# Attention kernel with a static instruction order: charging TensorE's tiling switches in the order's model, fillers in the tiling of their neighbours, projections through one bank, and the last unit by Ln and Exp

## The chip, the cores and the metric

The kernel runs on one core of one Trainium2 chip. The metric is the device time of one execution in microseconds (us). Every ratio compares runs of both kernels on the same chip in alternating rounds.

An execution is marked slow when it is over 1.5% above the fastest of the same kernel. With one core, that is the only sign of it. The granted TensorE clock in these traces is either 1.0 or 0.5 of full speed. I therefore use a second measure throughout, the **half-clock time** of an execution: twice (1 − mean granted clock) times the span. It says for how many microseconds TensorE ran at half speed.

Engines: TensorE (PE: matmuls; PEld: its weight loads), VectorE (DVE), ScalarE (ACT), GpSimd (POOL), SyncE (SP, issues the DMAs).

## The reference

Two attention layers on 2048 rows of width 512 with 32 heads of 16, outputs side by side. A is softmax attention and nearly all of the work. B is linear attention with softmax feature maps.

```python
def _A_ref(x, wqkv, wo):                      # x [1,2048,512] bf16
    qkv = (x @ wqkv).reshape(B, S, 3, H, Dh).transpose(2, 0, 3, 1, 4)
    q, k, v = qkv[0], qkv[1], qkv[2]
    p = softmax(einsum("bhqd,bhkd->bhqk", q, k) * Dh ** -0.5)
    o = einsum("bhqk,bhkd->bhqd", p, v)
    return o.transpose(0, 2, 1, 3).reshape(B, S, D) @ wo
# _B_ref (cut): phi = [softmax(x w_phi), softmax(-x w_phi)] for q and k;
#               o = phi_q (phi_k^T v) / (phi_q sum(phi_k) + 1e-6); o @ wo
return concatenate([a, b], axis=-1)
```

## The kernel before

Python decides the order of all instructions of every engine in advance. Each piece of work is a task with a modelled duration. A list scheduler takes the task that can start first and appends its instructions to its engine's list. Semaphores make the result correct whatever the true durations are, but the order is frozen: where the model is wrong, engines wait.

```python
    # in the scheduler: placing a task
        if self.filler is not None and t.eng == "pe":
            self.filler(self.free["pe"], start)      # zeros to keep TensorE busy
        t.end = start + t.dur + t.lat
        self.free[t.eng] = start + t.dur
```

A *unit* is 4 heads times 512 queries, and there are 32 units. Each unit has 16 key blocks. QK uses row tiling (4 row groups of 32), PV column tiling (4 groups of 32 columns), everything else the full array:

```python
    # QK: two row groups, one matmul each (a half-block of 1024 scores a partition)
    e.matmul(PS[:, b, :], KT[32*r:32*r+32, g, ...], QT[32*r:32*r+32, c, ...], start=True, stop=True,
             tile_position=(32 * r, 0))
    return _Task("pe", 0.3, pe_group(2, mm), ...)
    # PV: four column groups into bank 6; row 16 of each group becomes the softmax sum
    e.matmul(PS[32*r:32*r+32, 6, :], lhs(...), rhs(r), ..., tile_position=(0, 32 * r))
    t = _Task("pe", 0.25, emit, deps + ([xev[u - 1]] if u else []), ...)
```

The exponential of a half-block is made on one of two engines. On ScalarE it is one Exp into one of 7 score tiles `pT` (banks 0 to 3). On VectorE it is one conversion `rg<-PS` and then passes `rg<-rg` (the D banks, 4 and 5). The PV of a unit cannot start before the previous unit's bank 6 has been copied to X.

A filler puts zero matmuls, always on the full array, into the gaps that the model foresees on TensorE:

```python
    def fill(f, start):
        gap = start - f - 0.1
        ... # bank 6 while a PV group is open, else bank 7 if free
        while gap > 0.08:
            n = min(512, int((gap - 0.03) / 0.0004167) // 128 * 128)
            ... e.matmul(PS[:, bank, 0:n], zmv[:], rhs, ...)
            gap -= n * 0.0004167 + 0.03
```

The later K and Q projections run in pairs through both D banks, paced from 40 us on, one each 9 us. A unit ends with the division by its sums. The sums go out to DRAM, come back in another layout, a reciprocal is taken, it goes out and comes back broadcast, and GpSimd multiplies. Four output blocks follow, each through one bank, and then a check that all sums were in range, which writes a flag. The end of the program reads the flag and branches over a general version.

```python
            p1 = ... d_sum[u] <- X[16:128:32]        # 4 DMAs and a reciprocal
            p2 = ... Cs <- d_sum[u];   rc = reciprocal
            p3 = ... d_rec <- Cs;      p4 = ... Yd <- d_rec, broadcast
            mul[u] = ... pool: OT[:, g, :] = X * Yd
            if g == NG - 1: out_proj(c)              # 4 x (8 matmuls, copy, DMA), one bank
    ... # after the schedule: load all sums, three counts, flag
```

## Time and profile before

951.53 us, the median of 3 runs (951.09 to 953.96).

| stretch | length | what bounds it |
|---|---|---|
| body: start to the end of the last softmax Exp | 903.8 us | TensorE and ScalarE together to 700 us, then ScalarE |
| tail: from there to the end | 49.0 us | one serial chain |

First the busy times of the kernel before by stretch. The columns are the stretch, its length, busy time and (count) of PE, PEld, DVE, ACT and POOL, then the granted clock, the DMA share and GB/s.

```profile
core 0: us, PE busy (x) PEld busy (x) DVE busy (x) ACT busy (x) POOL busy (x), PEclk, DMA share, GB/s
40.00:100.00 60.00, 58.56 (x375) 15.93 (x378) 31.18 (x35) 49.61 (x55) 6.10 (x4) 1.00 0.02 6
...
300.00:400.00 100.00, 95.65 (x895) 27.84 (x900) 78.61 (x101) 83.61 (x98) 16.02 (x10) 0.95 0.05 14
...
700.00:800.00 100.00, 98.98 (x859) 27.25 (x859) 83.64 (x103) 97.85 (x107) 5.38 (x4) 1.00 0.06 18
```

TensorE looks full everywhere, but its fillers count as busy. ScalarE, whose work has no filler, is at 83% to 90% in the middle and 98% or more from 700 us on. VectorE is at 52% between 40 and 100 us.

The costliest groups of the kernel before (line, engine, operation, tiles, shapes, count; then busy us and mean ns of one; then idle time of the engine before them and what ended it):

```profile
L697 ACT ACTIVATE pT<-PS 128x1024 bf16<-128x1024 f32 x792 | 746.2, 1063 | 67.7 <-PE PS L595 47.4
...
L718 DVE TENSOR_SCALAR rg<-PS 128x1024 uint16<-128x1024 f32 x232 | 281.6, 1214 | 68.1 <-PE PS L587 67.2
...
L628 PE MATMUL PS<-zmv 128*128 128x512 bf16 (+3 forms) x498 | 145.9, 353 | 1.1 <-DVE zb L847 0.6
```

Of the 1024 half-blocks, 792 go to ScalarE and 232 to VectorE. From the waits list of ScalarE (total us, times, longest):

```profile
ACT pT L697 <- PE PS L595: 47.4, 18, 9.9
ACT pT L697 <- PE PS L587: 15.4, 38, 1.1
```

The 18 waits on PV (L595) are stalls with all seven score tiles full.

What a switch of tiling costs can be read off the timeline of the kernel before (start, duration shown, engine, line). The shown durations of matmuls overlap (0.40 us is shown where the next one starts after 0.32), so the starts are what to read:

```profile
501.44 0.40 PE L587 MATMUL PS<-QT,KT 32*128 32x512 bf16 x4
501.77 0.28 PE L628 MATMUL PS<-zmv 128*128 128x256 bf16 x1
501.98 0.39 PE L587 MATMUL PS<-QT,KT 32*128 32x512 bf16 x2
502.30 0.40 PE L595 MATMUL PS<-pT,VP 128*32 128x512 bf16 x4
```

From QK to PV is 0.32 us, where full-array fillers of 512 columns that follow each other start 0.215 us apart: about 0.1 us went into the change. The four QK matmuls on four row groups ran at once: the next matmul started 0.33 us after them, not four times 0.215. The 256-column filler took 0.21 us for about 0.107 us of streaming, half of the 0.215.

Last, the tail of the kernel before, from the timeline:

```profile
904.73 0.69 DVE L648 COPY X<-PS 128x512 f32<-128x512 f32 x1 [8.26 <-PE PS L595]
905.45 0.50 SPq L656 DMA_DIRECT2D d_sum<-X  x1
...
911.27 0.55 SPq L669 DMA_DIRECT2D Yd<-d_rec  x1
916.40 1.26 POOL L675 TENSOR_TENSOR OT<-X,Yd 128x512 bf16<-128x512 f32 x1 [18.80 <-DMA Yd<-d_rec]
...
918.12 3.91 PE L771 MATMUL PS<-WOp,OT 128*128 128x512 bf16 x7 [13.44 <-POOL OT L675]
...
922.07 0.69 DVE L775 CAST OA<-PS 128x512 bf16<-128x512 f32 x1 [13.08 <-PE PS L771]
...
933.85 0.69 DVE L775 CAST OA<-PS 128x512 bf16<-128x512 f32 x1 [2.70 <-PE PS L771]
...
935.33 0.39 SPq L1065 DMA_DIRECT2D sums<-d_sum  x1
...
941.81 2.29 DVE L1071 TENSOR_SCALAR_CACHE_REDUCE zb<-statR 128x2048 bf16<-128x2048 f32 x1
...
944.74 0.15 DVE L1077 TENSOR_SCALAR flag<-PS 1x1 int32<-1x1 f32 x1 [0.26 <-PE PS L1075]
```

Hardly anything in it overlaps. The matmuls of the first block (7 of 8 recorded) come about 0.55 us apart, those of the third and fourth 0.33: the clock had fallen to half at 909.8 us, 5 us after TensorE's last work, and came back at 926.8.

### The profile page before, as it was taken

To read this page: it belongs to the slowest core of one execution; us is meant where nothing else is said; L and a number is where in the kernel's file an instruction comes from. 1 tells how busy PE (TensorE), PEld (TensorE's weight loads), DVE (VectorE), ACT (ScalarE), POOL (GpSimd) and SP (SyncE) were. 2 spreads that over 40 slices of the span, in tenths; PEclk is the share of its full clock that TensorE was granted. 3 is DMA by queue.
4 is the path that set the end of the run, shared out by engine and by line. 5 is a ranking of instruction groups with operands and counts; after the bars stand their busy time and mean duration, and the time that the engine had idled before them with its cause. 6 is when DMAs were issued, how large, how long until landed. Compare 5 with 4: busy or idle time off the path is not lost.

```text
span 952.8 us, 17388 instructions
## 1 busy us (share of the span) xinstructions
PE 883.5 (93%) x7503; PEld 259.7 (27%) x7555; DVE 693.4 (73%) x867; ACT 796.3 (84%) x893; POOL 144.5 (15%) x121
## 2 busy tenths in 40 slices
PE   7999999999999999999999999999999999999931
PEld 3222222222222222332332223333222222222200
DVE  3346558998797687976986787887788689987502
ACT  5789958988898959998978799959999999999900
POOL 6500000123131220220220002212000001000000
PEclk9999999999999979999999999999999999999966
DMA  6000002332000000000000000000000000000000
GB/s 177 1 1 13 13 2 46 86 61 36 13 3 30 19 13 8 8 23 23 14 24 20 22 19 14 24 16 21 24 20 13 28 23 14 14 13 13 13 23 27
DMA packets 37375, 23.26 MB, mean 24 GB/s; under 512 B 23720, under 2 KB 32936, under 8 KB 37288
## 3 DMA queue, kind: packets, MB, share of 16 engines
q1 hardware_dynamic: 37288, 22.05, 8.8%
q8 instruction: 61, 1.00, 0.4%
q14 instruction: 26, 0.21, 0.1%
HBM read 14.17 MB, written 4.72 MB: 20 GB/s over the span
## 4 chain that ended last, share of the span: by engine, by line
PE 59%; ACT 26%; DVE 8%; issue 4%; DMA 2%; POOL 0%; POOLq 0%; SPq 0%
ACT pT L697 25%; PE PS L587 19%; PE PS L595 14%; PE PS L628 7%; PE PS L771 4%; PE PS L973 3%; PE PS L543 2%; DVE rg L729 2%; DVE rg L718 2%; PE PS L1041 2%; PE PS L906 2%; PE PS L485 2%; PE PS L878 1%; PE PS L488 1%; PE PS L992 1%
## 5 line engine op out<-in xcount | busy, mean ns | idle before, releaser
L697 ACT ACTIVATE pT<-PS 128x1024 bf16<-128x1024 f32 x792 | 746.2, 1063 | 67.7 <-PE PS L595 47.4
L587 PE MATMUL PS<-QT,KT 32*128 32x512 bf16 x2048 | 348.9, 384 | 8.6 <-ACT pT L697 4.0
L718 DVE TENSOR_SCALAR rg<-PS 128x1024 uint16<-128x1024 f32 x232 | 281.6, 1214 | 68.1 <-PE PS L587 67.2
L729 DVE TENSOR_SCALAR rg<-rg 128x2048 uint16<-128x2048 uint16 x348 | 245.1, 735 | 8.7 <-PE PS L595 5.0
L587 PEld LDWEIGHTS PS<-QT,KT 32*128 32x128 bf16 x2048 | 84.1, 91 | 271.9 <-ACT pT L697 169.4
L595 PE MATMUL PS<-pT,VP 128*32 128x512 bf16 x1584 | 148.6, 388 | 0.1
L628 PE MATMUL PS<-zmv 128*128 128x512 bf16 (+3 forms) x498 | 145.9, 353 | 1.1 <-DVE zb L847 0.6
L595 PE MATMUL PS<-rg,VJ 128*32 128x512 f16 x1392 | 126.8, 387 | 1.7 <-DVE rg L729 1.3
L675 POOL TENSOR_TENSOR OT<-X,Yd 128x512 bf16<-128x512 f32 x32 | 43.4, 1356 | 554.0 <-DMA Yd<-d_rec 546.0
L628 PEld LDWEIGHTS PS<-zmv 128*128 128x128 bf16 x498 | 38.6, 97 | 83.6 <-issue 74.7
L595 PEld LDWEIGHTS PS<-pT,VP 128*32 128x32 bf16 x1584 | 37.9, 94 | 85.5 <-issue 80.8
L771 PE MATMUL PS<-WOp,OT 128*128 128x512 bf16 x120 | 40.1, 413 | 18.4 <-POOL OT L675 13.4
L595 PEld LDWEIGHTS PS<-rg,VJ 128*32 128x32 bf16 x1392 | 34.2, 95 | 44.0 <-issue 25.2
L595 PE MATMUL PS<-rg,VP 128*32 128x512 f16 x464 | 45.9, 386 | 0.0
L775 DVE CAST OA<-PS 128x512 bf16<-128x512 f32 x16 | 11.1, 692 | 43.1 <-PE PS L771 43.1
L898 POOL TENSOR_TENSOR w<-zb,statR 128x1024 bf16<-128x1024 bf16 x16 | 32.9, 2056 | 59.9 <-DVE statR L896 59.9
L973 PE MATMUL PS<-xT,Wfq 128*128 128x512 bf16 x114 | 35.6, 384 | 4.1 <-issue 1.3
L1018 POOL TENSOR_TENSOR w<-w 128x512 f32<-128x512 f32 x16 | 20.4, 1278 | 119.9 <-DVE w L1004 119.9
L648 DVE COPY X<-PS 128x512 f32<-128x512 f32 x32 | 21.9, 683 | 11.0 <-PE PS L595 10.9
L887 ACT ACTIVATE zb<-PS 128x512 bf16<-128x512 f32 x32 | 17.4, 601 | 12.1 <-PE PS L878 12.0
L1044 DVE CAST w<-PS 128x1024 bf16<-128x1024 f32 x8 | 9.8, 1224 | 23.2 <-PE PS L1041 23.2
L543 PE MATMUL PS<-xT,w 128*128 128x512 bf16 x78 | 24.4, 384 | 1.7 <-issue 0.5
(87 smaller groups left out, 483.1 us busy)
## 6 DMA issues: line engine op xcount, KB each, us to landing
Yd<-d_rec SPq DMA_DIRECT2D x32, 256.0 KB
rg<-in_A_x_dram SPq DMA_DIRECT2D x4, 512.0 KB, 8.3
out_dram<-OA SPq DMA_DIRECT2D x16, 128.0 KB, 1.7
out_dram<-w SPq DMA_DIRECT2D x8, 256.0 KB, 2.2
w<-in_A_wqkv_dram SPq DMA_DIRECT2D x3, 512.0 KB, 6.0
WOp<-in_A_wo_dram SPq DMA_DIRECT2D x8, 64.0 KB, 7.8
d_sum<-X SPq DMA_DIRECT2D x32, 8.0 KB
Cs<-d_sum SPq DMA_DIRECT2D x32, 8.0 KB, 1.6
```

The source lines that it names most:

```text
L543: return e.matmul(PS[:, 4 + i // 4, :], w[:, ct, c0:c0 + 128], xT[:, ct, cc * 512:(cc + 1) * 512], start=(ct == 0), stop=(ct == 3))
L587: return e.matmul(PS[:, b, :], KT[32 * r:32 * r + 32, g, kt * 128:(kt + 1) * 128], QT[32 * r:32 * r + 32, c, g // 2, :], start=True, stop= ...
L595: return e.matmul(PS[32 * r:32 * r + 32, 6, :], lhs(8 * (g // 2) + 2 * r + g % 2), rhs(r), start=t.res["first"], stop=t.res["last"], tile_ ...
L628: P.op("pe", lambda e, n=n, rhs=rhs, bank=bank, first=first: e.matmul(PS[:, bank, 0:n], zmv[:], rhs, start=first, stop=first, skip_group_c ...
L648: xv = _Task("dve", 0.66, one("dve", lambda e, t: e.tensor_copy(X[:, t.res["x"].idx, :], PS[:, 6, :])), [], lat=0.1, need=[("x", x_sl, 1, 2)])
L675: mul[u] = put(po_n, _Task("pool", 1.55, one("pool", lambda e, t: e.tensor_tensor(OT[:, g, :], X[:, xi, :], Yd[:, yi(), :], ALU.mult)), [p ...
L697: return e.activation(pT[:, t.res["p"].idx, :], PS[:, b:b + 2, :].rearrange("p a n -> p (a n)"), ACT.Exp, scale=0.25)
L718: return e.tensor_scalar(rg[:, hold.res["i"].idx, 1024 * half:1024 * half + 1024], PS[:, 4:6, :].rearrange("p a n -> p (a n)"), ya, yb, AL ...
L729: ad = put(dv_ad, _Task("dve", 0.69, one("dve", lambda e, t, j=j: e.tensor_scalar(rg[:, t.res["j"].idx, :], rg[:, hold.res["i"].idx, :], f ...
L771: return e.matmul(PS[:, f.res["b"].idx, :], OT[:, g, st * 128:(st + 1) * 128], WOp[:, g, :], start=(g == 0), stop=(g == NG - 1))
L898: ph = put(po_phi, _Task("pool", 2.3, one("pool", lambda e, t, x0=x0, st=st: e.tensor_tensor(w[:, t.res["k"].idx, 0:1024].rearrange("p (g ...
L973: return e.matmul(PS[:, t.res["b"].idx, :], Wfq[:, ct, t8 * 128:(t8 + 1) * 128], xT[:, ct, cq * 512:(cq + 1) * 512], start=(ct == 0), stop ...
```

## The change

The intent has four parts. (1) The model charges 0.11 us whenever TensorE's next task has another tiling, and its durations become the streaming times. (2) A filler takes the tiling of a neighbour, so it adds no switch. (3) The later projections go one at a time through bank 7 and no longer hold the D banks. (4) The last unit skips the trip through DRAM. One fp32 matmul with a selection matrix broadcasts its sums, and ScalarE makes 1/sum as Exp(−Ln). The output of the other seven groups is accumulated meanwhile in the four free banks, and the checks of the earlier units move into the body.

```diff
+_SWITCH = 0.11
 # placing a task
+        dur = t.dur
+        if t.eng == "pe":
+            if self.filler is not None:
+                self.filler(self.free["pe"], start, self.kind, t.kind)
+            if t.kind != self.kind:
+                dur += _SWITCH
+            self.kind = t.kind
 # task costs (QK, PV, KV of B, dense)
-        return _Task("pe", 0.3, pe_group(2, mm), ...
+        return _Task("pe", 0.21, pe_group(2, mm), kind="qk", ...
-        t = _Task("pe", 0.25, emit, ...
+        t = _Task("pe", 0.22, emit, ..., kind="pv")
-                kt_ = _Task("pe", 0.26, pe_group(8, mp), ...
+                kt_ = _Task("pe", 0.21, pe_group(8, mp), ..., kind="pv",
 ... # dense: 0.22 -> 0.215 a matmul
 # fillers
-    def fill(f, start):
+    def fill(f, start, prev, nxt):
         gap = start - f - 0.1
+        kind = "pv" if "pv" in (prev, nxt) else prev
+        if kind != prev and kind != nxt:
+            gap -= _SWITCH
 ...
+            if kind == "pv":     # four 32-column matmuls, all 128 rows
+                return e.matmul(PS[32 * i:32 * i + 32, bank, 0:n], zmv[:, 0:32], ..., tile_position=(0, 32 * i))
+            if kind == "qk":     # one row group: 32 of 128 rows
+                return e.matmul(PS[:, bank, 0:n], zmv[0:32, :], ..., tile_position=(0, 0))
+            return e.matmul(PS[:, bank, 0:n], zmv[:], rhs(zmv[:]), **kw)
 # projections
-    def proj2(kind, g, c, nb):   ... # pairs in the D banks, from 40.0 + 9.0 * i
+    for g in (2, 3):
+        for c in range(4):
+            proj("k", g, c, M_bank)     # one bank, from 32.0
+        proj("q", g, 0, M_bank)
 ...
 # last unit
+        bc = put(pe_tl, ... matmul(PS[:, 4, :], sel[:], X[:, xi, :]) ...
+        for st in range(4):
+            for g in range(NG - 1):     # 28 matmuls into banks 0 to 3
+                f = put(pe_tl, ... matmul(PS[:, st, :], OT[:, g, ...], WOp[:, g, :], start=(g == 0), stop=False) ...
+        ln = put(ac_tl, ... activation(Yd[:, 0, :], PS[:, 4, :], ACT.Ln) ...
+        ex = put(ac_tl, ... activation(Yd[:, 0, :], Yd[:, 0, :], ACT.Exp, scale=-1.0) ...
+        ml = put(tl_d, ... OT[:, NG - 1, :] = X * Yd ...
+        ... # 4 matmuls, copies on two engines, 2 DMAs, flag
```

(Cuts are marked by "..."; the counts that feed the flag are left out.)

## The prediction

> **What bounds it now.** (1) The body, 0 to 904.2 us, where the last softmax Exp ends. Busy times by stretch: from 100 to 700 us TensorE is 94 to 97% busy, ScalarE 84 to 90%, VectorE 75 to 87%; from 700 us ScalarE is 98 to 100%. ScalarE's waits sum to about 90 us between 40 and 700 us; the waits list puts 47.4 us, in 18 waits, on the PV matmuls: seven score tiles are full and PV cannot run, because a unit's last VectorE blocks or a projection in the D banks are late. (2) The tail, 48.6 us serial. Timeline: X copy 904.7, four DMA hops to 916.4, GpSimd multiply 1.26, 32 output matmuls with copies through one bank until 934.5 (half of them at half clock, 0.55 us each), sums loaded by 940.3, checks, flag at 944.9, then 7.9 us of branch and end.
>
> **A tiling switch.** Starts in the trace: two QK matmuls before PV take 0.318 us, four PV before QK 0.333, two dense before QK 0.538; the streaming is 0.213 (dense 0.43). So 0.105 to 0.12 us per change. [...] The old model charges 0.30, 0.25 and 0.44; over 804 QK, 541 PV and 222 dense stretches some 80 us of TensorE time are unknown to the static order. 317 filler stretches in full-array mode add some 460 switches, about 49 us, mostly inside waits.
>
> **Tail after (estimate from those durations).** X copied at 905.4; fp32 broadcast matmul 1.0; 28 accumulating matmuls behind it 6.0, 4 more 0.9 at full clock; Ln, Exp, multiply (0.6, 0.6, 0.7) end near 909, hidden behind the 28. Copies end 914.5; flag 915.5; plus 7.9: 923.4. Gain 29 us, all critical. The clock should stay full: before, it halved at 909.8, 5 us after TensorE went idle [...].
>
> **Body after.** Single-bank projections free the D banks early: the stalls near 46, 68, 127 and 160 us (about 20 us) lie there, and VectorE converts only 6 half-blocks from 40 to 100 us. Recovered ScalarE time is shared with VectorE blocks, about 0.7 us per us; with more early VectorE work, 15 us. An order that fits TensorE's true time, and fillers without switches: 10 us. Not cured: VectorE costs that the model has wrong (scalar_tensor_tensor 1.17 us against 0.2 charged, in the stall near 623 to 634), and TensorE's load from 200 to 400 us.. Body gain 25 us, uncertain by 20.
>
> **Predicted: 900 us, 872 to 926. Faster by over 2%: 0.94; within 2%: 0.05; slower: 0.01.**
>
> **Right or wrong, by step.** Last Exp to end: about 19 us, not 48.6; no half clock there; Ln and Exp 0.6 us each, no new table load. The first projections end near 110 us, not 143.6. VectorE does more than 232 half-block conversions, ScalarE fewer than 792 Exps; ScalarE's waits on PV drop from 47 to about 25 us. Fillers between QK and QK cost 0.21 us per 512 columns without 0.1 gaps.
>
> **What would make it wrong.** Fillers on one row group or in 32-column tiles let the granted clock fall inside the body (before: one dip, at 333 us); one projection bank delays K and Q; new unit-boundary stalls; a table load; a slow broadcast matmul.

(The streaming time of 0.213 us is 512 columns at the 0.0004167 us a column of the filler's own code; in the trace such matmuls start 0.215 us apart. The trace of the kernel before holds no fp32 matmul and no Ln, so the 1.0 and 0.6 us for these were my estimates, as was the 0.7 us per us. In the trace of the kernel after, the matmul that follows the fp32 one starts 0.96 us behind it, and the Ln takes 0.60 us. That the clock would stay full was inferred from the one fall at 909.8 us.)

## More of the kernel before

The sets of experiments ran on four chips. Where absolute times of different sets stand side by side, note that the kernel before, at 36 us of half-clock time, took 950.5 to 952.7 us on all four.

The records give the mean clock to three digits, so a half-clock time is known to about 1 us.

## The result, and the profile after

914.53 us, the median of 4 runs (912.73 to 916.70), beside 952.75 us of the kernel before (4 runs). Ratio 0.9597, 95% interval 0.9562 to 0.9631. Here and below a ratio is the mean time of one kernel's fast runs over that of the other's of the same rounds, so it is not quite the ratio of the medians.

| | before | after | difference |
|---|---|---|---|
| span of the profiled run | 952.8 | 911.9 | −40.9 |
| body | 903.8 | 891.8 | −12.0 |
| tail | 49.0 | 20.1 | −28.9 |
| half-clock time in the body | 10.2 | 47.8 | +37.6 |
| ScalarE idle in the body after 20 us | 98.0 | 101.1 | +3.1 |

(The prediction read 904.2 and 48.6 us for the body and the tail of the kernel before; by the trace it is 903.8 and 49.0.)

The tail of the kernel after, from the timeline:

```profile
892.43 0.69 DVE L658 COPY X<-PS 128x512 f32<-128x512 f32 x1 [3.59 <-PE PS L589]
...
893.77 1.13 PE L833 MATMUL PS<-X,sel 128*128 128x512 f32 x2
...
894.73 6.21 PE L838 MATMUL PS<-WOp,OT 128*128 128x512 bf16 x28
...
894.93 0.60 ACT L843 ACTIVATE Yd<-PS 128x512 f32<-128x512 f32 x1 [3.11 <-PE PS L833]
895.56 0.63 ACT L845 ACTIVATE Yd<-Yd 128x512 f32<-128x512 f32 x1
896.22 0.69 DVE L848 TENSOR_TENSOR OT<-X,Yd 128x512 bf16<-128x512 f32 x1 [1.64 <-ACT Yd L845]
900.56 0.74 PEld L852 LDWEIGHTS PS<-WOp,OT 128*128 128x128 bf16 x4
900.77 1.03 PE L852 MATMUL PS<-WOp,OT 128*128 128x512 bf16 x4
...
903.38 0.14 DVE L873 TENSOR_SCALAR flag<-PS 1x1 int32<-1x1 f32 x1 [0.26 <-PE PS L870]
```

The product is ready at 896.9, but the four matmuls that need it start at 900.8, behind the 28. As predicted, TensorE's queue bounds the tail, at full clock (0.22 us a matmul), and Ln and Exp need no table load: they take 0.60 and 0.63 us, 0.03 us apart, and the only load in the trace is at 0.8 us (1.28 us long), as in the kernel before.

The busy times of the kernel after, same columns as before:

```profile
40.00:100.00 60.00, 58.07 (x472) 14.60 (x470) 54.01 (x73) 47.62 (x52) 6.63 (x5) 1.00 0.02 7
...
300.00:400.00 100.00, 94.45 (x1008) 28.57 (x1007) 79.57 (x104) 85.46 (x101) 20.98 (x13) 0.98 0.03 10
400.00:500.00 100.00, 95.26 (x856) 30.80 (x855) 79.13 (x103) 77.63 (x92) 17.73 (x15) 0.93 0.05 18
...
700.00:800.00 100.00, 96.19 (x910) 25.56 (x909) 84.57 (x104) 98.22 (x108) 6.69 (x5) 1.00 0.06 21
```

VectorE is at 90% between 40 and 100 us. In the middle ScalarE has gained nothing: between 100 and 700 us it is busy for 519 us before and after, with 78% from 400 to 500 us, where the granted clock averages 0.93.

The groups of the kernel after (L712 is the Exp, L733 VectorE's conversion, L631 the one-row-group filler, L628 the 32-column one), and ScalarE's waits:

```profile
L712 ACT ACTIVATE pT<-PS 128x1024 bf16<-128x1024 f32 x784 | 735.4, 1100 | 72.8 <-PE PS L589 54.4
...
L733 DVE TENSOR_SCALAR rg<-PS 128x1024 uint16<-128x1024 f32 x240 | 291.4, 1214 | 59.3 <-PE PS L581 58.0
...
L631 PE MATMUL PS<-zmv 32*128 32x512 bf16 (+3 forms) x252 | 64.8, 349 | 0.6 <-ACT zb L1067 0.5
...
L628 PE MATMUL PS<-zmv 128*32 128x512 bf16 (+3 forms) x620 | 47.0, 349 | 1.4 <-DVE QT L528 0.7
```

```profile
ACT pT L712 <- PE PS L589: 54.4, 15, 9.0
ACT pT L712 <- PE PS L581: 15.3, 31, 1.6
```

ScalarE's waits on PV went up from 47.4 to 54.4 us. The body is shorter because ScalarE has less to do: 15 us less busy time, from 8 fewer Exps and 4 fewer copies of K above all. The granted clock tells why more was not gained. It is part 2 of the page, 40 equal slices, tenths of full speed; first the kernel before:

```profile
PEclk9999999999999979999999999999999999999966
```

and the kernel after:

```profile
PEclk9999999799999999988999999999899999999978
```

Before, there is one dip in the body, at 333 us. After, there are six, which sum to 47.8 us. In two of them TensorE was busy throughout (kernel after, windows placed on the half-clock stretches at 404.7 and 865.5 us, same columns as above):

```profile
404.70:415.00 10.30, 10.30 (x64) 3.45 (x62) 6.40 (x10) 0.60 (x1) 2.33 (x2) 0.50 0.00 0
...
865.50:875.70 10.20, 10.20 (x74) 2.25 (x70) 4.95 (x6) 8.20 (x9) 0.00 (x0) 0.50 0.10 28
```

In the first, ScalarE worked 0.6 us out of 10.3. In the 4.7 us ahead of it TensorE was busy for 4.31. The chain of waits of the kernel after shows there what half clock does (start, us, what):

```profile
403.99 1.30 PE PS L631 x5
405.30 0.13 PE PS L581 x2
405.42 4.57 PE PS L631 x12
```

TensorE's list is fixed, so the fillers stand between one QK and the next. At half clock they take twice the time that they were made for (512-column fillers on one row group that follow each other start 0.427 us apart there, 0.216 at full clock), and they are then themselves on the critical chain.

### The profile page after: what moved, and what is told of

Read it like the earlier page. It is cut to its first block, busy times and chain, and to the rows that moved or that the text cites. A ratio compares the mean times of both kernels' runs of the same rounds, so it can differ in the third digit from the quotient of the medians.

```text
span 911.9 us, 18351 instructions
## 1 busy us (share of the span) xinstructions
PE 861.8 (95%) x7990; PEld 252.8 (28%) x7990; DVE 709.4 (78%) x912; ACT 783.7 (86%) x885; POOL 144.7 (16%) x123
## 4 chain that ended last, share of the span: by engine, by line
ACT 46%; PE 44%; DVE 6%; issue 1%; DMA 1%; SPq 0%
ACT pT L712 45%; PE PS L581 13%; PE PS L589 10%; PE PS L1058 4%; PE PS L511 4%; PE PS L786 3%; DVE rg L733 2%; PE PS L508 2%; PE PS L991 2%; DVE rg L744 1%; PE PS L631 1%; PE PS L628 1%; PE PS L1125 1%; PE PS L965 1%; ACT zb L972 1%
## 5 line engine op out<-in xcount | busy, mean ns | idle before, releaser
L712 ACT ACTIVATE pT<-PS 128x1024 bf16<-128x1024 f32 x784 | 735.4, 1100 | 72.8 <-PE PS L589 54.4
L581 PE MATMUL PS<-QT,KT 32*128 32x512 bf16 x2048 | 359.7, 390 | 21.7 <-ACT pT L712 11.5
L733 DVE TENSOR_SCALAR rg<-PS 128x1024 uint16<-128x1024 f32 x240 | 291.4, 1214 | 59.3 <-PE PS L581 58.0
L744 DVE TENSOR_SCALAR rg<-rg 128x2048 uint16<-128x2048 uint16 x360 | 251.5, 726 | 17.6 <-PE PS L589 14.6
L589 PE MATMUL PS<-rg,VJ 128*32 128x512 f16 x1440 | 134.5, 393 | 0.3 <-DVE rg L744 0.2
L631 PE MATMUL PS<-zmv 32*128 32x512 bf16 (+3 forms) x252 | 64.8, 349 | 0.6 <-ACT zb L1067 0.5
L628 PE MATMUL PS<-zmv 128*32 128x512 bf16 (+3 forms) x620 | 47.0, 349 | 1.4 <-DVE QT L528 0.7
L511 PE MATMUL PS<-xT,w 128*128 128x512 bf16 x128 | 38.5, 384 | 2.3 <-DVE KT L529 1.3
L786 PE MATMUL PS<-WOp,OT 128*128 128x512 bf16 x96 | 29.1, 384 | 0.6
L631 PEld LDWEIGHTS PS<-zmv 32*128 32x128 bf16 x252 | 23.7, 97 | 19.0 <-issue 3.8
L529 DVE TENSOR_SCALAR KT<-PS,hmask 128x512 bf16<-128x512 f32 x28 | 19.7, 745 | 6.7 <-PE PS L511 6.6
```

The lines of the kernel that those rows point to most:

```text
L511: return e.matmul(PS[:, t.res["b"].idx, :], w[:, ct, c0:c0 + 128], xT[:, ct, c * 512:(c + 1) * 512], start=(ct == 0), stop=(ct == 3))
L581: return e.matmul(PS[:, b, :], KT[32 * r:32 * r + 32, g, kt * 128:(kt + 1) * 128], QT[32 * r:32 * r + 32, c, g // 2, :], start=True, stop= ...
L589: return e.matmul(PS[32 * r:32 * r + 32, 6, :], lhs(8 * (g // 2) + 2 * r + g % 2), rhs(r), start=t.res["first"], stop=t.res["last"], tile_ ...
L628: return e.matmul(PS[32 * i:32 * i + 32, bank, 0:n], zmv[:, 0:32], rhs(zmv[:]), tile_position=(0, 32 * i), **kw)
L631: return e.matmul(PS[:, bank, 0:n], zmv[0:32, :], rhs(zmv[0:32, :]), tile_position=(0, 0), **kw)
L712: return e.activation(pT[:, t.res["p"].idx, :], PS[:, b:b + 2, :].rearrange("p a n -> p (a n)"), ACT.Exp, scale=0.25)
```

## The experiments

The theory (A), to be tested: the granted clock falls because of the fillers on one row group, which use 32 of 128 rows (in fill_full's record because of those in 32 columns too), TensorE then holds up ScalarE, and that costs more than the saved switches. It was a guess: the trace had shown the dips, not their cause. The rival (B): the dips come from TensorE waiting for VectorE, whatever the filler. Fillers do not influence the model's times, so kernels that differ in fillers alone have the same order of all other work. I compared the instruction lists of every engine, and they are equal but for the zero matmuls. All runs below gave correct results.

| run | median us | ratio to before (95%) | half-clock us, fast runs |
|---|---|---|---|
| after_again | 912.76 | 0.9548 (0.9500 to 0.9595) | 31 to 57 |
| fill_full | 921.17 | 0.9568 (0.9511 to 0.9624) | 49 to 57 (three slow runs 98 to 124) |
| fill_mixed | 902.24 | 0.9456 (0.9411 to 0.9502) | 7 to 36 |
| tail_only | 924.70 | 0.9684 (0.9646 to 0.9723) | 7 to 19 |
| fill_cols | 896.53 | 0.9388 (0.9331 to 0.9445) | 7 to 16 |
| proj_old_mixed | 918.12 | 0.9599 (0.9525 to 0.9674) | 22 to 44 |
| model_old_mixed | 913.02 | 0.9559 (0.9486 to 0.9631) | 15 to 40 |
| order_control | 900.78 | 0.9438 (0.9380 to 0.9497) | 11 to 25 |
| fill_rows | 956.01 | 0.9984 (0.9947 to 1.0021) | 150 to 176 |
| dve_costs | 909.95 | 0.9553 (0.9518 to 0.9589) | 5 to 26 |
| dve_costs_tail | 908.43 | 0.9531 (0.9511 to 0.9551) | 7 to 26 |
| cols_tail | 895.06 | 0.9402 (0.9380 to 0.9425) | 5 to 18 |

The medians are over all runs of a kernel (fill_full has three slow ones of 6, fill_rows one of 4, tail_only one of 7, proj_old_mixed one of 5); the ratios are over fast runs alone. The kernel before had 32 to 64 us in its fast runs. In its trace 33 us of that lie in the tail. In the traces of the others the tail's share is 6 to 11 us, nearly all of it after the flag.

### after_again: the changed kernel, unaltered

> The changed kernel unaltered, so that the others of this set are compared with it on the same chip. Both theories: ratio to before 0.960 as already measured, within 0.005; half-clock stretches in the body that sum to roughly 48 us, as in the first trace of it, most of them after stretches of fillers on one row group (32 of 128 rows).

Its half-clock time ranged from 31 to 57 us and its time from 905.5 to 915.1 us, the two rising together. The ratio, 0.9548, lies just outside the 0.955 to 0.965 that was expected. Four of the six stretches begin at nearly the same places as in the first trace (172, 350, 404, 449 us). That most of them follow one-row-group fillers did not hold: in both traces three of six do, by the matmul records of the 3.4 us ahead of each. Ahead of those at 172, 350 and 449 us no such filler ran, and TensorE streamed for only 1.1 to 1.7 us of the 3.4.

### fill_full: every filler on the full array

```diff
-        kind = "pv" if "pv" in (prev, nxt) else prev
+        kind = None
```

> Same order of all work as the changed kernel; only the fillers go back to the full-array tiling (each then costs switches that were not allowed for). Theory A [...]: half-clock time in the body falls from about 48 us to under 15 us and the kernel is faster than the changed one by 5 to 12 us. Rival B (the dips come from TensorE waiting for VectorE whatever the filler, and the filler's tiling saves its switches): the dips stay, and the kernel is 3 to 10 us slower than the changed one.

Neither theory had this right. The half-clock time did not fall (49 to 57 us in fast runs, 98 to 124 in the slow ones), and at equal half-clock time the kernel is as fast as the changed one: 914.0 us at 56.6, against 914.2 us at 56.6. So the switches that the change saves in its fillers are worth nothing measurable. The expectation had one thing wrong about the edit: with it, the code does allow for a switch (0.11 us of the gap), which leaves less filler: 44.9 us of streaming (columns counted in the trace, at the 0.0004167 us a column of the filler's own code) against 70.1 in the changed kernel. Of those 70.1, however, 42.3 are on one row group.

### fill_mixed: full array only where one row group was used

```diff
-        kind = "pv" if "pv" in (prev, nxt) else prev
+        kind = "pv" if "pv" in (prev, nxt) else None
```

> Same order again; fillers beside PV keep the 32-column tiling (all 128 rows busy), only those between QK and QK, or between QK and dense work, use the full array instead of one row group. Theory A, with the one-row-group form as the culprit: half-clock time in the body under 15 us and 5 to 14 us faster than the changed kernel, at least as good as fill_full. Rival B: dips as in the changed kernel, time within 3 us of it or slower by up to 5 us for the extra switches.

10.5 us faster than the changed kernel in the same rounds, with 7 to 36 us at half clock. This supports A in the form that it names, the one-row-group filler. Its trace has 13.7 us of half clock in the body, under the 15 that were expected; its worst run, with 36 us in all, must have had more. It has 58.4 us of filler, all on 128 rows.

### fill_cols: every filler in the 32-column tiling

```diff
-        kind = "pv" if "pv" in (prev, nxt) else prev
+        kind = "pv"
```

> Same order as the changed kernel; every filler in the 32-column tiling with all 128 rows busy, those between QK and QK too (fill_mixed has the full array there and had 7 to 36 us of half clock over its six runs, the changed kernel 31 to 57 in the same set). Theory A1 (what lowers the clock is the one-row-group filler, which keeps 32 of 128 rows busy; any form that keeps all rows busy will do): half-clock time and time as in fill_mixed, about 902 us, 7 to 36 us at half clock. Rival A2 (the full-array form itself holds the clock up, the 32-column form doesn't): half-clock time 40 us or more and about 912 us.

896.5 us, 7 to 16 us at half clock: A1, and somewhat better than it expected. The full-array form is not needed. That a filler keeps all rows busy is not enough by itself, though: in fill_full every filler does, and the clock dips as before (49 to 57 us at half clock). ScalarE's longest wait group in the trace of fill_cols:

```profile
ACT pT L712 <- PE PS L589: 51.8, 15, 9.0
```

### fill_rows: every filler on one row group

```diff
-        kind = "pv" if "pv" in (prev, nxt) else prev
+        kind = "qk"
```

> Same order as the changed kernel; every filler in the one-row-group form. Dose test of the theory that this form lowers the granted clock: half-clock time well above the changed kernel's 31 to 59 us, over 80 us, and so at the slope seen within each kernel (0.33 to 0.45 us lost per us at half clock, from 894 us at full clock) over 922 us. Rival (fill_cols gained for another reason): half-clock time 31 to 60 us and 905 to 917 us.

Ratio 0.9984, the whole gain of the change gone. The three fast runs took 948.3, 953.6 and 958.4 us, with 150 to 176 us at half clock; a slow one took 982 us, with 251. From the median of fill_cols to the median of these fast runs, the fillers' form alone moves this kernel by 57 us. The granted clock in the pages of fill_cols and then fill_rows:

```profile
PEclk9999999999899999999999999999999999999998
```

```profile
PEclk9999999998999978979999995797999999967767
```

The 27 fast runs of the five kernels that share one order (the changed kernel, in two sets, fill_full, fill_mixed, fill_cols, fill_rows) lie on one straight line, fitted by least squares: **time = 894.4 us + 0.36 × half-clock time**, with no run more than 2.5 us off it. The slow runs of these kernels, which were not fitted, lie within 3.1 us of it too. Within these 2.5 us, then, the filler's form acts through the clock alone.

What stood ahead of the clock's falls can be read off the kept traces; this reading was made after the experiments. In the clock records the changes of one trace lie whole multiples of 3.41 us apart: the half-clock stretches in the bodies of before and after last 3.41, 6.83, 10.24 or 13.65 us, the full-clock stretches between them 34.1 to 566.6. For each window of 3.41 us on that grid between 20 and 880 us, in all 14 traces, I summed what I call the row share: the time in which TensorE streamed columns, weighted with the rows in use out of 128, over the length of the window. The clock fell to half after 41 of 3409 windows at full clock. All 41 had a row share of at most 0.383. Every window under 0.364 was followed by half clock (29), and none above 0.383; of the 31 in between, 12 were. (The traces of before and after have 7 of the 41, at 0.30 to 0.36.) The share of time in which any matmul streamed does not part them: it was up to 0.77 ahead of a fall and down to 0.40 without one. Of the windows at half clock, none under 0.67 was followed by the full clock, and every one above 0.734 was. So in these traces a busy TensorE was not enough to keep the clock full, and the row share parts the windows better; no run varied it alone, so what the clock follows is not shown. (Some matmul records are missing from a trace, 8 of the 128 output matmuls in that of the kernel before, so a share is good to a few per cent.) This covers fill_full too. It has 5 full-clock windows with a row share under 0.38, fill_mixed and fill_cols have 1 each, the changed kernel 10 and 8 in its two traces, and fill_rows 14. Rival B keeps a part: where TensorE waits and no filler stands, the row share falls as well (to 0.35, 0.30 and 0.36 ahead of the dips at 172, 350 and 449 us).

### tail_only: the kernel before with the new last unit

Everything but the last unit and its checks is as before; the order is the same up to the end.

```diff
-_SWITCH = 0.11
+_SWITCH = 0.0
 ... # old task costs, old fillers, old projections
```

> The kernel before with the new last unit alone (old task costs, old fillers, old projections; the order of TensorE's work is the same as before up to the very end). Theory (the tail is worth 28 us by itself, the body the rest): ratio to before 0.970, that is about 924 us, span from last Exp to end about 20 us. Rival (the tail is worth more, and the body's change gives little or nothing): ratio 0.960, as the whole change.

Ratio 0.9684, 924.7 us. Its fastest run, at 7 us half clock, took 921.7 us. The kernel before took 950.5 to 952.7 us at 36 us half clock, which is the level of its tail alone with hardly a dip in the body. The tail is worth 29 to 31 us, and the rival is out: from 921.7 to 896.1 us (fill_cols at 7 us half clock), 26 us come from the body.

### proj_old_mixed and model_old_mixed: one part of the body undone

Both start from fill_mixed, so that half clock disturbs little.

```diff
 # proj_old_mixed
-    for c in range(4):
-        proj("k", 1, c, M_bank)
 ...
+        proj2(kind, g, c, 40.0 + 9.0 * i)      # pairs in the D banks, as before
```

> fill_mixed with the old projections (pairs in the two D banks, paced from 40 us on every 9 us). Theory from the prediction (the projections in one bank of their own are worth about 15 of the body's 25 us): about 15 us slower than fill_mixed at the same half-clock time, so about 915 us; VectorE makes about 6 half-block conversions from 40 to 100 us instead of 17. Rival (the projections are worth under 5 us, because VectorE's early work is only moved): 900 to 907 us.

```diff
 # model_old_mixed
-_SWITCH = 0.11
+_SWITCH = 0.0
-        return _Task("pe", 0.21, pe_group(2, mm), kind="qk", ...
+        return _Task("pe", 0.3, pe_group(2, mm), kind="qk", ...
 ... # PV 0.22 -> 0.25, KV 0.21 -> 0.26, dense 0.215 -> 0.22; fillers keep their 0.11
```

> fill_mixed with the old task costs in the order's model and no charge for a switch (fillers keep their own allowance for switches). Theory (the truer model is worth about 10 us at full clock): about 912 us at the half-clock time of fill_mixed. Rival 1 (the true costs buy nothing beyond noise of the order): within 5 us of fill_mixed. Rival 2 (the model is most of the gain): 920 us or more. Since the old model sees fewer and other gaps, fillers fall elsewhere and the half-clock time may differ; compare at equal half-clock time.

The fitted lines of the fast runs, read at 20 us half-clock time (for proj_old_mixed and tail_only 2 us outside their runs): fill_mixed 901.4, proj_old_mixed 913.4, model_old_mixed 911.6, tail_only 926.5 us. The projections are worth about 12 us (15 was expected), the truer model about 10. Together they make 22 of the 25 us between tail_only and fill_mixed, and the rest was not taken apart. VectorE's work on its exponentials (tile `rg`) between 40 and 100 us, first in proj_old_mixed, then in fill_cols, whose order is that of fill_mixed (columns: PE, PEld, DVE):

```profile
40.00:100.00 60.00, 3.64 (x44) 0.98 (x44) 14.13 (x16) 1.00 0.02 6
```

```profile
40.00:100.00 60.00, 9.68 (x112) 2.23 (x112) 34.08 (x39) 1.00 0.02 7
```

This agrees with the predicted mechanism: the D banks are free early.

### order_control: an equally true model, another order

```diff
-_SWITCH = 0.11
+_SWITCH = 0.10
```

> fill_mixed with the charge for a switch 0.10 instead of 0.11 us: a model as true as before, but the order of the work differs from early on. It measures how much the order alone moves the time. Theory (differences of 10 us between these kernels are effects of what was changed): within 5 us of fill_mixed at the same half-clock time. Rival (any change of the order moves the time by 10 us): 10 us or more away.

902.3 us at 20 us half clock, 0.9 us from fill_mixed, although the order differs from early on. That is one draw of a new order, and it speaks against chance. It does not settle it: dve_costs, below, is another new order, and it is 11 us slower for a reason that stayed open. So the 10 and 12 us are what these two edits brought in the orders that came of them. That they are due to the truer costs and the freed banks is supported, the banks by VectorE's early work, but not shown.

### dve_costs: the model's VectorE costs as the trace has them

Based on fill_cols.

```diff
-                z1 = put(dv_y, _Task("dve", 0.2, ... scalar_tensor_tensor
+                z1 = put(dv_y, _Task("dve", 1.17, ...
-            return put(dv_ev, _Task("dve", 0.66, ...
+            return put(dv_ev, _Task("dve", 0.69 if par is None else 0.75, ...
```

> fill_cols with VectorE costs in the model as the trace has them: 1.17 us instead of 0.2 for the scalar_tensor_tensor, 0.75 and 0.69 instead of 0.66 for the copies of K and of Q and V. Theory from the prediction (unit-boundary stalls of ScalarE, such as the one near 623 to 634 us before, come from VectorE costs that the model has wrong, and are left by the change): ScalarE waits of over 1 us, 74 us in fill_cols, fall below 60 us, and the kernel is 4 to 10 us faster than fill_cols, 887 to 893 us. Rival (the stalls come from the order itself, one PV bank and seven score tiles, not from the costs): within 4 us of fill_cols, stalls as before.

A plain miss: 910 us, about 11 us slower than fill_cols at the same half-clock time (907.3 against 896.1 us at 7.2), so outside the rival's 4 us too. ScalarE's waits of over 1 us rose from 74 to 86 us. The stalls at 60, 87, 118, 275 and 340 us sit where they sat. The prediction's reading of this instruction was wrong as well, as two lines of the timeline of the kernel before show:

```profile
625.37 1.27 POOL L1018 TENSOR_TENSOR w<-w 128x512 f32<-128x512 f32 x1 [11.84 <-DVE w L1004]
625.45 1.24 DVE L1013 SCALAR_TENSOR_TENSOR zs<-zs 128x32 f32<-128x32 f32 x1
```

The VectorE instruction on 32 columns ends 0.05 us after GpSimd's addition ends. In the trace of before, 14 of the 16 look so, and one more ends 0.05 us after GpSimd's multiplication. One had no GpSimd work beside it and took 0.19 us. The waits list shows nothing of this: the time is inside the shown duration, 1.23 to 1.25 us in the 15. By the 15 of 16, 1.17 us is not a fixed cost of the instruction but mostly time beside GpSimd, which depends on the order, and a fixed 1.17 is no truer than 0.2. What holds the instruction up was not shown. Why the order that came of it is 11 us worse, I did not settle.

### dve_costs_tail and cols_tail: the broadcast matmul in a stream of its own

```diff
+    pe_bc = SC.stream("pe", 8)
-        bc = put(pe_tl, ...
+        bc = put(pe_bc, ...
```

In the changed kernel TensorE ran fillers while X was copied (until 893.1 us) and began the broadcast at 893.8, because the broadcast stood first in one queue with the 28 matmuls. With a stream of its own, the first 6 of the 28 run in that time.

> dve_costs with the broadcast matmul of the last unit in a stream of its own, so that the first accumulating output matmuls run while X is still being copied, in place of fillers; all else in the same order. In the changed kernel TensorE held fillers and idle from the last PV at 892.2 us to the broadcast at 893.8. Theory (TensorE's queue of 28 + 4 matmuls is what bounds the tail): 1 to 2 us faster than dve_costs. Rival (the chain through Ln, Exp and multiply bounds it): no change or up to 1 us slower.

> The best of the parts: fill_cols (every filler in the 32-column tiling) with the broadcast matmul in a stream of its own; the VectorE costs of the model stay as they were. Order as in fill_cols up to the tail. From the parts: fill_cols at 896.5 us less the 1.5 us that the timelines of dve_costs and dve_costs_tail show between the last Exp and the flag: 895 us, ratio to before about 0.938, 7 to 16 us at half clock, last Exp to flag about 10.2 us instead of 11.7. Rival (the gain of 1.5 us is only there because X is late in that order): 896 to 898 us.

From the last Exp to the end of the flag: 11.7 us in dve_costs, 10.2 us in dve_costs_tail, so the 1.5 us are there in the timeline; in cols_tail it is 10.2 us too, as expected. The medians differ by 1.5 us too, but the intervals of the ratios overlap. cols_tail came out at 895.06 us, ratio 0.9402, as expected; its profiled run has no half clock in the body at all. It is the fastest kernel by its median, 6% under the kernel before and 18 to 20 us under the changed one. Over fill_cols, which ran on another chip, the gain is not clear of noise: the two ratios are 0.9402 and 0.9388.

## Why the prediction was right or wrong

- **The total: 900 us predicted, 872 to 926 as the range, 914.5 measured.** Inside the range, 14.5 us above its centre.
- **The tail: right.** 29 us predicted, 28.9 in the spans, 29 to 31 by tail_only. The parts were right too: the 28 matmuls bound it, and the clock stays full to the flag. (After the flag, where TensorE has no work, 7.6 us at half clock follow, so "no half clock there" does not hold to the very end.) The 28 started about 1.5 us later than they could, as cols_tail shows.
- **The body: "Body gain 25 us".** That is what the order gives at full clock: 26 us from tail_only to fill_cols at 7 us half clock each. What was measured in the profiled run is 12 us. The missing term is the clock. By the line above, the changed kernel's half-clock times of 31 to 59 us cost 9 to 19 us over fill_cols' 7. The prediction named this under "What would make it wrong" and gave it no us in the sum.
- **"no half clock there": right for the tail up to the flag.** The prediction had one observation for it, the fall at 909.8 us, 5 us after TensorE's last work. In the body that observation gave no warning: there the clock stayed at half for 10.3 us with TensorE busy for all 10.3.
- **The split of the 25 us.** Projections: 15 expected, about 12 measured. "An order that fits TensorE's true time, and fillers without switches: 10 us": undoing the order's costs alone lost about 10. The fillers without switches gave nothing at equal half-clock time (fill_full), although the step "0.21 us per 512 columns" held: one-row-group fillers start 0.216 us apart after one another and 0.226 after QK.
- **"The first projections end near 110 us": wrong.** They end at 129.6 us, against 143.6 before; one bank carries them all.
- **"ScalarE's waits on PV drop from 47 to about 25 us": wrong.** 54.4 us after, and still 51.8 us in fill_cols, which has 7 us of half clock in the body of its trace. The step that failed is the recovery of the early stalls. Before, the Exps waited at 46, 68, 127 and 160 us for 19.5 us together; after, at 41, 60, 87 and 116 us for 17.8 us. The gain came by work moving to VectorE (240 conversions against 232, 17 against 6 between 40 and 100 us). In fill_cols the body is 28.2 us shorter than before; ScalarE is busy 17.6 us less and idle 10.5 us less, and none of that is from its waits on PV. That the sum still came out at 25 to 26 us is in part luck.
- **"Not cured: VectorE costs that the model has wrong": the cure fails.** See dve_costs. At least one of the stalls that stay has another cause: in fill_cols the longest wait on PV, 9.0 us from 274.8 us on, has TensorE at work on output projections placed ahead of PV.

What stays open: what sets the granted clock (the row share parts the windows, but no run varied it alone); how much of the 10 and 12 us is the order that happened to come; and why one order with other VectorE costs is 11 us worse.

## What to carry to other kernels

When instructions exist only to keep an engine's clock up, judge them by the granted clock they produce, not by the time that they save: here the one-row-group form, which fits QK without a switch, lost 57 us when every filler had it. Compare variants at equal half-clock time, or the clock's scatter will be read as an effect of the edit. A serial tail read off the timeline could be costed to about a microsecond. The gain from a better order came near its estimate in sum, but not by the waits that the estimate rested on.
